# Band attention with a gated MLP on one core: negative tau through Q's scale, token sums on two engines, out products by column halves

## The chip, the cores and the metric

The kernel runs on 1 core of one Trainium2 chip. The time is that of the device, in microseconds (us), of one execution of the whole kernel; lower is better. The engines are named as in the profile: PE (TensorE, matrix products), PEld (its weight loads), DVE (VectorE), ACT (ScalarE), POOL (GpSimd) and SP (SyncE, which issues the DMAs).

## What is computed

The reference, cut to what matters:

```python
scale = 1.0 / np.sqrt(64)                                  # q, k, v: 8 batches, 8 heads, 576 rows, 64
scores = scale * q @ k^T
scores = where(scores >= max(scores) - tau, scores, -1e9)  # per row
attn = exp(scores - max(scores));  attn /= attn.sum() + 1e-9
x = (attn @ v).transpose(0, 2, 1, 3).reshape(4608, 512)
gate = sigmoid(x @ w_gate);  val = x @ w_val               # w: 512 x 1536
out = (gate * val) @ w_out                                 # 1536 x 512
```

Only scores within tau of the row's largest take part in the softmax. With a negative tau no score does, all are -1e9, and the row becomes the plain mean of v.

## The kernel before

**Attention.** There are 32 visits, one for each batch and pair of heads (name `b_hp`: `1_0` is batch 1, pair 0). A visit has 576 queries for each of two heads, in 9 tiles of 128 queries by 576 keys: four full tiles of each head, in groups of two, and one tile of both heads' 64 leftover queries. For each tile PE makes scores (L618), DVE their maximum (L625), ACT the exponent (L639), DVE masks and sums (L642; the sums land in a small tile `sm`). Then `normalise` (L665): the denominators are changed by `den_t` on ACT (L668), or on POOL (L671) in the first 18 tiles, DVE takes the reciprocal (L674), POOL computes (p + w_t) * sm (L687). `w_t` is 1 for a negative tau and 0 otherwise, and `den_t` is 576 * w_t + 1e-9, so that a negative tau gives the mean. PE transposes p (L702). In the first `NPV` = 4 visits the product with v is plain fp32 (L790). In the others p and v are split into a high and a low half (ACT rounds p to the high half, L712, DVE subtracts it, L719) and three cheaper products are summed (L803). The query scale goes into Q by ACT.

**The MLP**, all of it in such halves. The weights come through 36 conversions of a tile of 128 rows (`convert`, L401): among other steps three DVE operations (L441, L445, L451), a cast on ACT and a low half on POOL (L469), on DVE for the tiles in `DVE_LO_OUT`. Tokens of batches 0 to 4 run block by block (`in_units`: m, L861; `out_units`: o, L899). Batches 5 and 6, and 7 with all the leftovers, go as two token pairs, k = 0 and 1, through a scheme that makes four products of halves from seven (p1, p5, p6, p2, p7, p4, p3) of sums: weight sums on POOL (`sums`, from L940, spread by `SUMS` over the matmul units of earlier blocks), and token sums (`token_sums`, L993): `put` rounds a sum to its high half on ACT (L999) and DVE subtracts for the low one (L1001), `less` makes the next sum on POOL (L1006). `in_two` makes the q products (L1092; banks qa, qb, qc), `out_two` the r products (L1146; banks ra, rb, rc). Products p1 and p2 add up in bank a, p6, p7 and p4 in b, p5 and p3 in c; after a product DVE folds the bank into a partial result (`chains`, L1031 for r), before the next product of that bank may go on. In `out_two` a product has three groups g of two ff tiles, each with one load of weights (L1135), and two column halves e with banks of their own. The sums of every second product share buffers, so those of one are written when those of the one before are used up.

**What sets the order.** Every operation is handed to a planner (`Plan`) with its engine, an estimated cost and a key. It goes through time and gives each free engine the ready operation of the smallest key that finds a buffer (`SLOTS`), and so fixes one static instruction stream for each engine. Attention keys count tiles; MLP blocks come behind them on PE and fill what attention leaves free. `LEAD` is how far ahead a visit's loads and casts are keyed, `CONV_IN` the keys of the weight conversions (first, step), `SHIFT` an offset of the keys of all visits from the fifth on, `PAD` one more such number, `AHEAD_TWO` = 8 how many units before their use out weights may be loaded.

Of the kernel before, what the change touches and what calls it, by code (L numbers as in the profile page):

```python
# [19 lines left out]
def f32(ap):  # L20
    return ap.bitcast(F32)
# [21 lines left out]
class Plan:  # L43
# [157 lines left out]
    "w": 7, "t2": 5,  # L201
}
LEAD = 8
CONV_IN, CONV_OUT = (8, 2.2), (24, 3)
# [30 lines left out]

DEN_UNTIL = 18
NORM_ACT = ()
# [3 lines left out]
SHIFT = 30  # L241
# [6 lines left out]
DVE_LO_IN, DVE_LO_OUT = (), ()  # L248
# [9 lines left out]
SUMS = (36, 4)  # L258

AWAY = 1  # L260
AHEAD_TWO = 8


def act(n):
    return 0.19 + 0.0008 * n
# [15 lines left out]
def kernel(  # L281
# [57 lines left out]
    ntau_t = cp.tile([P, 1], F32, tag="ntau", name="ntau_t")  # L339


    w_t = cp.tile([P, 1], F32, tag="w", name="w_t")
    den_t = cp.tile([P, 2], F32, tag="den", name="den_t")
    nc.vector.tensor_scalar(out=w_t, in0=tau_t, scalar1=0.0, scalar2=None, op0=ALU.is_ge)
    nc.vector.tensor_scalar(out=w_t, in0=w_t, scalar1=-1.0, scalar2=1.0, op0=ALU.mult, op1=ALU.add)
    for i in range(2):
        nc.vector.tensor_scalar(
            out=den_t[:, i : i + 1], in0=w_t, scalar1=float(S), scalar2=1e-9, op0=ALU.mult, op1=ALU.add
        )
    nc.vector.tensor_scalar(out=ntau_t, in0=w_t, scalar1=1e38, scalar2=None, op0=ALU.mult)  # L350
    nc.vector.tensor_tensor(out=ntau_t, in0=ntau_t, in1=tau_t, op=ALU.subtract)
# [132 lines left out]
    class Visit:  # L484
# [39 lines left out]
        def split_scores(self, key, n):  # L524
# [15 lines left out]
            op("ACT", act(W), key, lambda: nc.scalar.activation(q2.ap[:, 0], qn.ap, AF.Copy, scale=QSCALE),  # L540
# [5 lines left out]
                out=q2.ap[:, 1], in0=qn.ap, scalar=QSCALE, in1=f32(q2.ap[:, 0]), op0=ALU.mult, op1=ALU.subtract  # L546
# [16 lines left out]
        def plain_scores(self, key, n):  # L563
# [17 lines left out]
            if len(heads) == 1:  # L581
                op("ACT", act(W), key, lambda: nc.scalar.activation(qn.ap, qn.ap, AF.Copy, scale=QSCALE), writes=[qn])
                return
            for i, c in enumerate((slice(0, WM), slice(WM, 2 * WM), slice(2 * WM, W))):
                op("ACT", act(c.stop - c.start), key, lambda c=c: nc.scalar.activation(
                    qn.ap[:, c], qn.ap[:, c], AF.Copy, scale=QSCALE
                ), writes=[(qn, i)])
# [59 lines left out]
    class Group:  # L647
        def __init__(self, vis, h, tiles):
# [7 lines left out]
            self.sm = buf("sm", [P, 2 * n], F32, f"sm{self.name}")  # L656
# [8 lines left out]
        def normalise(self, key):  # L665
            sm, p, n = self.sm, self.p, self.n
            if DEN(self.vis.first) == "ACT":
                op("ACT", 0.3, key, lambda: nc.scalar.activation(sm.ap[:, :n], sm.ap[:, :n], AF.Identity, bias=den_t[:, 0:1]),  # L668
                   writes=[sm])
            else:  # L670
                op("POOL", 0.3, key, lambda: nc.gpsimd.tensor_tensor(  # L671
                    out=sm.ap[:, :n], in0=sm.ap[:, :n], in1=den_t[:, :n], op=ALU.add
                ), writes=[sm])
            op("DVE", 0.17, key, lambda: nc.vector.reciprocal(out=sm.ap[:, :n], in_=sm.ap[:, :n]), writes=[sm])  # L674
            if NORM(self.vis.first) == "ACT":

                op("ACT", 0.3, key, lambda: nc.scalar.activation(
                    sm.ap[:, n:], sm.ap[:, :n], AF.Copy, scale=w_t[:, 0:1]
                ), writes=[sm])
                for i in range(n):  # L680
                    op("ACT", 0.74, key, lambda i=i: nc.scalar.activation(
                        p.ap[:, i * S : (i + 1) * S], p.ap[:, i * S : (i + 1) * S], AF.Identity,
# [519 lines left out]
    t = 0  # L1202
# [165 lines left out]
```

## Time and profile before

| what | value |
|---|---|
| median of 3 runs | 1405.61 us (1403.37 to 1407.85) |
| the profiled execution | 1396.95 us |
| its span, first to last instruction | 1395.2 us |
| TensorE clock granted in it | 0.999 |

One profiled execution gives, for each engine, which instruction ran when, how long, and what ended the idle time ahead of it. A row of a group reads: line, engine, operation, output <- input, shape, count | busy us, mean ns of one | idle us before, and which engine and line ended it. A row of the timeline reads: start, length, engine, line, what, [idle before <- who ended it]. "issue" is idle time that no recorded wait explains. Rows that take part in the argument are shown in the prediction.

### The profile page before, as it was taken

What the parts mean: (1) busy time and instruction counts of PE and PEld (TensorE: products, weight loads), DVE (VectorE), ACT (ScalarE), POOL (GpSimd) and SP (SyncE); (2) the same over time, 40 slices, a digit from 0 to 9 for tenths busy, and PEclk for the clock granted to TensorE, in tenths of its full rate; (3) what the DMA queues carried; (4) which work ended last, traced back from release to release, by engine and by line L of the source; (5) the groups of instructions that cost most, each with busy time, mean ns of one, the idle gap of its engine ahead of it and who ended that gap; (6) DMA issues with size and microseconds to landing.
All of it is one profiled execution on the core that took longest, in us unless ns stands there. A gap on an engine that the chain in (4) does not pass through costs nothing.

```text
span 1395.2 us, 23257 instructions
## 1 busy us (share of the span) xinstructions
PE 1357.9 (97%) x7472; PEld 1154.2 (83%) x7472; DVE 1097.0 (79%) x2144; ACT 875.3 (63%) x1930; POOL 801.4 (57%) x868
## 2 busy tenths in 40 slices
PE   7998999999999999999999999999999999899998
PEld 5666788888888888888888888888888887788886
DVE  7997989888788888888888888888936559645595
ACT  6877777677777777777777777777732235322242
POOL 5888765448787777786777976455420137001160
PEclk9999999999999999999999999999999999999999
DMA  7889888869999998899988999776567666665574
GB/s 266 279 248 314 303 260 238 230 205 264 267 261 330 292 278 250 261 289 296 304 267 242 303 295 277 200 224 198 160 223 227 201 195 202 202 199 187 184 225 137
DMA packets 142328, 341.28 MB, mean 245 GB/s; under 512 B 22784, under 2 KB 42752, under 8 KB 142208
## 3 DMA queue, kind: packets, MB, share of 16 engines
q1 hardware_dynamic: 142064, 339.80, 79.8%
q8 instruction: 61, 1.00, 0.3%
q14 instruction: 59, 0.48, 0.1%
q10 hardware_dynamic: 144, 0.00, 0.0%
HBM read 232.78 MB, written 55.57 MB: 207 GB/s over the span
## 4 chain that ended last, share of the span: by engine, by line
PE 78%; DMA 6%; DVE 6%; POOL 3%; ACT 2%; issue 2%; SPq 1%; DVEq 0%; ACTq 0%; POOLq 0%
PE m L861 17%; PE o L899 11%; PE s L618 9%; PE av L803 8%; PE qb L1092 7%; PE tp L702 6%; PE qa L1092 4%; PE qc L1092 4%; DMA su<-wid 4%; PE rb L1146 3%; PE av L790 2%; PE ra L1146 2%; PE rc L1146 2%; PE s_l L618 2%; POOL su L947 1%
## 5 line engine op out<-in xcount | busy, mean ns | idle before, releaser
L861 PE MATMUL m<-x,wi 128*128 128x512 f32 x1152 | 314.0, 403 | 0.0
L687 POOL TENSOR_SCALAR p<-p,w_t,sm 128x576 f32<-128x576 f32 x256 | 216.8, 857 | 91.5 <-DVE sm L674 80.7
L861 PEld LDWEIGHTS m<-x,wi 128*128 128x128 f32 x1152 | 200.9, 189 | 30.9
L642 DVE SCALAR_TENSOR_TENSOR p<-s,st,p 128x576 f32<-128x576 f32 x256 | 206.2, 812 | 23.0 <-ACT p L639 18.6
L625 DVE TENSOR_REDUCE st<-s 128x1 f32<-128x576 f32 x256 | 190.4, 751 | 34.1 <-PE s L618 30.1
L899 PE MATMUL o<-g,wo 128*128 128x512 f32 x720 | 194.3, 403 | 0.0
L639 ACT ACTIVATE p<-s,st 128x576 f32<-128x576 f32 x256 | 188.8, 738 | 6.9 <-DVE st L625 5.4
L712 ACT CAST pt<-tp 128x512 fp32r<-128x512 f32 x224 | 128.2, 587 | 63.5 <-PE tp L702 59.4
L719 DVE TENSOR_TENSOR pt<-tp,pt 128x512 fp32r<-128x512 f32 x224 | 150.5, 684 | 18.3 <-ACT pt L712 16.3
L618 PE MATMUL s<-kd,qd 128*128 128x288 f32 x896 | 159.7, 301 | 4.9 <-DVE p L642 2.7
L618 PEld LDWEIGHTS s<-kd,qd 128*128 128x128 f32 x896 | 136.8, 188 | 23.0 <-issue 3.0
L702 PE MATMUL tp<-ident,p 128*128 128x128 f32 x1024 | 146.8, 273 | 1.9 <-ACT pl_l L737 1.4
L899 PEld LDWEIGHTS o<-g,wo 128*128 128x128 f32 x720 | 126.1, 189 | 20.6 <-PE tp_l L702 0.2
L803 PE MATMUL av<-pt,vs 128*128 128x320 f32 (+1 forms) x896 | 137.0, 295 | 1.7 <-DVE pt L719 1.7
L702 PEld LDWEIGHTS tp<-ident,p 128*128 128x128 f32 x1024 | 122.3, 140 | 19.1 <-issue 3.2
L803 PEld LDWEIGHTS av<-pt,vs 128*128 128x128 f32 x896 | 129.2, 188 | 9.1 <-POOL p L687 2.1
L1006 POOL TENSOR_TENSOR gA<-gA 128x512 f32<-128x512 f32 x12 | 16.2, 1347 | 206.4 <-DVE gA L1071 206.4
L883 POOL TENSOR_TENSOR g<-th,g 128x512 fp32r<-128x512 f32 x60 | 78.8, 1313 | 23.0 <-ACT g L881 21.4
L806 ACT COPY avt<-av 64x256 f32<-64x256 f32 x112 | 44.2, 394 | 58.2 <-PE av L803 56.4
L1029 DVE TENSOR_TENSOR qu<-qb,qp 128x512 f32<-128x512 f32 x48 | 33.2, 691 | 55.9 <-PE qb L1092 48.4
L807 DVE TENSOR_TENSOR xf<-av,avt 64x256 f32<-64x256 f32 x112 | 50.8, 453 | 32.3 <-ACT avt L806 31.1
L749 DVE TENSOR_TENSOR pl<-lk,pl 64x128 fp32r<-64x128 f32 x224 | 64.7, 289 | 13.8 <-ACT pl L746 7.3
(171 smaller groups left out, 2743.1 us busy)
## 6 DMA issues: line engine op xcount, KB each, us to landing
wi<-wid SPq DMA_DIRECT2D x96, 512.0 KB, 7.1
kd<-k SPq DMA_DIRECT2D x112, 320.0 KB, 8.1
wo<-wod SPq DMA_DIRECT2D x60, 512.0 KB, 7.6
qd<-q SPq DMA_DIRECT2D x112, 128.0 KB, 6.1
wid<-ws SPq DMA_DIRECT2D x24, 512.0 KB, 4.5
su<-wid SPq DMA_DIRECT2D x24, 512.0 KB, 7.9
sid<-su SPq DMA_DIRECT2D x24, 512.0 KB, 4.6
wa<-wid SPq DMA_DIRECT2D x24, 512.0 KB, 4.5
```

The lines of the kernel that those rows point to most:

```text
L618: nc.tensor.matmul(s.ap[:, c, :HALF], st(), mv(slice(k0 + c * HALF, k0 + (c + 1) * HALF)), start=m == 0, stop=m == len(steps) - 1,)
L625: op("DVE", 0.76, key, lambda: nc.vector.tensor_reduce(out=st.ap[:, 0:1], in_=sv(), axis=AX.XY, op=ALU.max, negate=True), reads=[s], write ...
L639: op("ACT", 0.74, key, lambda: nc.scalar.activation(p(), sv(), AF.Exp, bias=st.ap[:, 0:1], scale=1.0), reads=[s, (st, 0)], writes=[(g.p, i)])
L642: op("DVE", 0.9, key, lambda: nc.vector.scalar_tensor_tensor(out=p(), in0=sv(), scalar=st.ap[:, 1:2], in1=p(), op0=ALU.is_ge, op1=ALU.mult ...
L687: op("POOL", 0.9, key, lambda i=i: nc.gpsimd.tensor_scalar(out=p.ap[:, i * S : (i + 1) * S], in0=p.ap[:, i * S : (i + 1) * S], scalar1=w_t ...
L702: nc.tensor.matmul(tp.ap[:, c, :], self.p.ap[:, o + c * P : o + (c + 1) * P], ident, is_transpose=True, start=c == 0, stop=c == NJ - 1, sk ...
L712: op("ACT", 0.58, key, lambda: nc.scalar.copy(hi(), tp.ap), reads=[tp], writes=[(self.pt, (0, i))])
L719: op("DVE", 0.69, key, lambda: nc.vector.tensor_tensor(out=lo(), in0=tp.ap, in1=f32(hi()), op=ALU.subtract), reads=[tp, (self.pt, (0, i))] ...
L803: nc.tensor.matmul(av.ap, st, mv, start=i == 0, stop=i == len(ms) - 1)
L861: nc.tensor.matmul(m.ap, wv[:, a, c * P : (c + 1) * P], xs[c].ap[:, z, c0:c1], start=e == 0, stop=e == 11,)
L899: nc.tensor.matmul(acc.ap, wv[:, f, a], g[fg * ND + f].ap[:, z], start=(fg, f, a, z) == (0, 0, 0, 0), stop=(fg, f, a, z) == (NFG - 1, ND - ...
L1092: nc.tensor.matmul(acc.ap, wv[:, y, (2 * h + c) * P : (2 * h + c + 1) * P], xt[prod][c].get()[:, z], start=e == 0 and prod in FIRST, stop= ...
```

## The change

Scale and denominators: Q is multiplied by a `[128, 1]` tile `scale_t` (the query scale for tau >= 0, else 0), so that a negative tau makes all scores 0 and every one passes the threshold 0; `ntau_t` is -max(tau, 0). `w_t` and `den_t` go, and with them L668, L671 and the second operand of L687; the reciprocal follows L642 directly. Token sums: the low halves (L1001) take their engine in turn, DVE, DVE, POOL. `out_two`: a product issues its three loads first, and all products but p1 then run column half by column half. One more visit (1_0) has the plain fp32 product with v (`NPV`). A third partial of the chains lies in the slot `pc` where it lay in `t2`, and `t2` has 6 slots. The weight sums come once in 6 units, three low halves of out weights go to DVE, and `LEAD`, `CONV_IN`, `PAD` and `SHIFT` have other values, by which the planner orders anew. Dead code goes.

```diff
@@ SLOTS and numbers @@
-    "w": 7, "t2": 5,
+    "w": 7, "t2": 6,
-LEAD = 8
-CONV_IN, CONV_OUT = (8, 2.2), (24, 3)
+LEAD = 3
+CONV_IN, CONV_OUT = (12, 2.2), (24, 3)
-PAD = 56
-NPS, NPV = 4, 4
+PAD = 64
+NPS, NPV = 4, 5
-SHIFT = 30
+SHIFT = 20
-DVE_LO_IN, DVE_LO_OUT = (), ()
+DVE_LO_IN, DVE_LO_OUT = (), range(6, 12, 2)
-SUMS = (36, 4)
+SUMS = (36, 6)
+TURNS = ("DVE", "DVE", "POOL")
@@ setup @@
-    nc.vector.tensor_scalar(out=w_t, in0=tau_t, scalar1=0.0, scalar2=None, op0=ALU.is_ge)
-    nc.vector.tensor_scalar(out=w_t, in0=w_t, scalar1=-1.0, scalar2=1.0, op0=ALU.mult, op1=ALU.add)
...
+    nc.vector.tensor_scalar(out=ntau_t, in0=tau_t, scalar1=0.0, scalar2=-1.0, op0=ALU.max, op1=ALU.mult)
+    nc.vector.tensor_scalar(out=scale_t, in0=tau_t, scalar1=0.0, scalar2=QSCALE, op0=ALU.is_ge, op1=ALU.mult)
@@ Visit.prepare (the same for qn.ap, and as the scalar of q2's low half on DVE) @@
-            op("ACT", act(W), key, lambda: nc.scalar.activation(q2.ap[:, 0], qn.ap, AF.Copy, scale=QSCALE),
+            op("ACT", act(W), key, lambda: nc.scalar.activation(q2.ap[:, 0], qn.ap, AF.Copy, scale=scale_t[:, 0:1]),
@@ Group.normalise @@
-            if DEN(self.vis.first) == "ACT":
-                op("ACT", 0.3, key, lambda: nc.scalar.activation(sm.ap[:, :n], sm.ap[:, :n], AF.Identity, bias=den_t[:, 0:1]),
-                   writes=[sm])
...
-            op("DVE", 0.17, key, lambda: nc.vector.reciprocal(out=sm.ap[:, :n], in_=sm.ap[:, :n]), writes=[sm])
+            op("DVE", 0.17, key, lambda: nc.vector.reciprocal(out=sm.ap, in_=sm.ap), writes=[sm])
             for i in range(n):
                 op("POOL", 0.9, key, lambda i=i: nc.gpsimd.tensor_scalar(
-                    out=p.ap[:, i * S : (i + 1) * S], in0=p.ap[:, i * S : (i + 1) * S], scalar1=w_t[:, 0:1], scalar2=sm.ap[:, i : i + 1],
-                    op0=ALU.add, op1=ALU.mult,
+                    out=p.ap[:, i * S : (i + 1) * S], in0=p.ap[:, i * S : (i + 1) * S],
+                    scalar1=sm.ap[:, i : i + 1], scalar2=None, op0=ALU.mult,
                 ), reads=[sm], writes=[(p, i)])
@@ token_sums, put @@
-            op("DVE", 0.69, key, lambda: nc.vector.tensor_tensor(
+            e = next(turns)
+            op(e, {"DVE": 0.69, "POOL": 1.3}[e], key, lambda: {"DVE": nc.vector, "POOL": nc.gpsimd}[e].tensor_tensor(
                 out=to.get()[:, 1], in0=src.get(), in1=f32(to.get()[:, 0]), op=ALU.subtract
@@ chains @@
-        t = {c: buf("pc" if c == "u3" and tag == "q" else "t2", [P, SM], F32, f"{tag}{c}{n}") for c in ("p1", "u2", "u3")}
+        t = {c: buf("pc" if c == "u3" and not (tag == "r" and n.endswith("_1")) else "t2", [P, SM], F32, f"{tag}{c}{n}") for c in ("p1", "u2", "u3")}
@@ out_two @@
         for prod in SEVEN:
+            ws = []
             for g in range(NFG):
                 w = buf("w", [P, 2, 2, 2, P], F32R, f"wo2{k}_{prod}_{g}")
...
-                for e in range(2):
+                ws.append(w)
+            for g, e in [(g, e) for g in range(NFG) for e in range(2)] if prod == "p1" else [(g, e) for e in range(2) for g in range(NFG)]:
+                if True:
+                    w = ws[g]
                     bank, t, after = quads[e]
...
                     if g == NFG - 1:
                         after(prod)
-                unit_ends.append(end)
+                if e or prod != "p1":
+                    unit_ends.append(end)
```

How this moves instructions shows at three places. First, PE in the first pair's output products, where p7 ends and p4 begins (rb0_0 and rb0_1 are bank b of column halves 0 and 1; gs0_p7_* are token sums of product p7, q2 and ptc being its last two; wo20_p7_1 the weights of group 1). Before:

```order
L1146 MATMUL rb0_0_14752<-gs0_p7_q2_14824,wo20_p7_2_14805 128x512 x3
L1146 MATMUL rb0_0_14752<-gs0_p7_ptc_14830,wo20_p7_2_14805 128x512 x3
L1146 MATMUL rb0_0_14752<-gs0_p4_0_14846,wo20_p4_0_14826 128x512 x3
L1146 MATMUL rb0_0_14752<-gs0_p4_1_14850,wo20_p4_0_14826 128x512 x3
L1146 MATMUL rb0_0_14752<-gs0_p4_2_14866,wo20_p4_1_14848 128x512 x3
L1146 MATMUL rb0_0_14752<-gs0_p4_3_14870,wo20_p4_1_14848 128x512 x3
L1146 MATMUL rb0_0_14752<-gs0_p4_4_14883,wo20_p4_2_14868 128x512 x3
L1146 MATMUL rb0_0_14752<-gs0_p4_5_14887,wo20_p4_2_14868 128x512 x3
L1146 MATMUL rb0_1_14767<-gs0_p7_0_14782,wo20_p7_0_14761 128x512 x6
L1146 MATMUL rb0_1_14767<-gs0_p7_1_14803,wo20_p7_1_14784 128x512 x6
```

The bank rb0_0 goes from p7 straight to p4. Changed:

```order
L1121 MATMUL rb0_0_14512<-gs0_p7_q2_14679,wo20_p7_2_14593 128x512 x3
L1121 MATMUL rb0_0_14512<-gs0_p7_ptc_14683,wo20_p7_2_14593 128x512 x3
L1121 MATMUL rb0_1_14553<-gs0_p7_1_14584,wo20_p7_1_14590 128x512 x6
L1121 MATMUL rb0_1_14553<-gs0_p7_q2_14679,wo20_p7_2_14593 128x512 x3
L1121 MATMUL rb0_1_14553<-gs0_p7_ptc_14683,wo20_p7_2_14593 128x512 x3
L1121 MATMUL rb0_0_14512<-gs0_p4_0_14629,wo20_p4_0_14644 128x512 x3
L1121 MATMUL rb0_0_14512<-gs0_p4_1_14632,wo20_p4_0_14644 128x512 x3
L1121 MATMUL rb0_0_14512<-gs0_p4_2_14642,wo20_p4_1_14646 128x512 x3
L1121 MATMUL rb0_0_14512<-gs0_p4_3_14648,wo20_p4_1_14646 128x512 x3
```

Between the end of p7 in rb0_0 and the start of p4 there now stand 12 matmuls of rb0_1.

Second, POOL in the same stage (gA and gB are gated activations of which `less` makes sums, gs their halves, xb and xs those of the second pair's tokens). Before:

```order
L1006 TENSOR_TENSOR gA0_5_14200<-gB0_5_14222,gA0_5_14200 128x512
L1006 TENSOR_TENSOR gA0_8_14338<-gB0_8_14360,gA0_8_14338 128x512
L1006 TENSOR_TENSOR gA0_9_14477<-gB0_9_14499,gA0_9_14477 128x512
L1006 TENSOR_TENSOR xb1_2_0_13795<-xb1_2_0_13795,xb1_0_0_13431 128x512
L1006 TENSOR_TENSOR gB0_0_13823<-gB0_0_13823,gA0_0_13793 128x512
L1006 TENSOR_TENSOR gB0_1_13945<-gB0_1_13945,gA0_1_13923 128x512
L1006 TENSOR_TENSOR gB0_4_14083<-gB0_4_14083,gA0_4_14061 128x512
L1006 TENSOR_TENSOR gB0_5_14222<-gB0_5_14222,gA0_5_14200 128x512
L1006 TENSOR_TENSOR gB0_8_14360<-gB0_8_14360,gA0_8_14338 128x512
L1006 TENSOR_TENSOR gB0_9_14499<-gB0_9_14499,gA0_9_14477 128x512
L1006 TENSOR_TENSOR xb1_3_0_13762<-xb1_3_0_13762,xb1_1_0_13741 128x512
```

Changed, the second part of it:

```order
L972 TENSOR_TENSOR gs0_p2_3_14527<-gB0_5_14018,gs0_p2_3_14527 128x512
L977 TENSOR_TENSOR gB0_5_14018<-gB0_5_14018,gA0_5_13996 128x512
L977 TENSOR_TENSOR gB0_8_14156<-gB0_8_14156,gA0_8_14134 128x512
L972 TENSOR_TENSOR gs0_p7_1_14584<-gA0_4_13857,gs0_p7_1_14584 128x512
L977 TENSOR_TENSOR gA0_9_14273<-gB0_9_14295,gA0_9_14273 128x512 x2
L977 TENSOR_TENSOR gB0_9_14295<-gB0_9_14295,gA0_9_14273 128x512
L972 TENSOR_TENSOR xs1_p2_0_14392<-xb1_2_0_13529,xs1_p2_0_14392 128x512
L972 TENSOR_TENSOR gs0_p4_1_14632<-gB0_1_13741,gs0_p4_1_14632 128x512
L972 TENSOR_TENSOR gs0_p4_4_14658<-gB0_8_14156,gs0_p4_4_14658 128x512
L977 TENSOR_TENSOR xb1_2_0_13529<-xb1_2_0_13529,xb1_0_0_13177 128x512
L977 TENSOR_TENSOR xb1_3_0_13501<-xb1_3_0_13501,xb1_1_0_13477 128x512
L972 TENSOR_TENSOR gs0_p7_ptc_14683<-gA0_9_14273,gs0_p7_ptc_14683 128x512
```

Low halves (L972) now stand between the sums (L977), and the last low half of p7 (gs0_p7_ptc) is POOL's, behind two sums for the second pair.

Third, SP where block 0's gate and value weights end (wid11_1 is the last of these tiles in DRAM, wi0_11_1a its load for block 0, qd1_3 and kd1_3 the scaled queries and keys of visit 1_3, in pieces). Before:

```order
L474 DMA wid11_1_131<-ws11_1_2495 128x1024
L840 DMA wi0_11_0a_2532<-wid11_0_130 128x1024
L555 DMA qd1_3_0_2615<-q21_3_2605 64x512
L840 DMA wi0_11_1a_2623<-wid11_1_131 128x1024
L559 DMA kd1_3_0_2630<-k21_3_2595 64x2x640 x2
L528 DMA kn2_0_2642<-in_k_dram 128x640
L840 DMA wo0_0_0_2660<-wod0_132 128x1024
L534 DMA qn2_0_2673<-in_q_dram 128x640
L555 DMA qd1_3_0_2615<-q21_3_2605 64x512
L555 DMA qd1_3_1_2704<-q21_3_2605 64x512 x2
```

Changed:

```order
L808 DMA wi0_10_1a_2550<-wid10_1_124 128x1024
L808 DMA wi0_11_0a_2605<-wid11_0_125 128x1024
L501 DMA vn2_0_2620<-in_v_dram 128x640
L1222 DMA xa1_1_139<-xf1_1_2176 128x512
L1229 DMA xp1_1_135<-xf1_1_2176 256x1x32
L460 DMA wid11_1_126<-ws11_1_2597 128x1024
L808 DMA wi0_11_1a_2719<-wid11_1_126 128x1024
L520 DMA qn2_0_2730<-in_q_dram 128x640
L541 DMA qd1_3_0_2385<-q21_3_2372 64x512
L808 DMA wo0_0_0_2744<-wod0_127 128x1024
L541 DMA qd1_3_1_2510<-q21_3_2372 64x512
```

The write of wid11_1 now stands directly ahead of the load that waits for it, with a piece of qd1_3_0 two rows behind that load; before, two rows lay between write and load, and that piece stood five behind.

More of the change, by code (lines that the diff above doesn't have):

```diff
@@ L1 @@
 import heapq
+import itertools
 from contextlib import ExitStack
@@ L339 @@
     ntau_t = cp.tile([P, 1], F32, tag="ntau", name="ntau_t")
-    w_t = cp.tile([P, 1], F32, tag="w", name="w_t")
-    den_t = cp.tile([P, 2], F32, tag="den", name="den_t")
-    nc.vector.tensor_scalar(out=w_t, in0=tau_t, scalar1=0.0, scalar2=None, op0=ALU.is_ge)
-    nc.vector.tensor_scalar(out=w_t, in0=w_t, scalar1=-1.0, scalar2=1.0, op0=ALU.mult, op1=ALU.add)
[L346 to L351, printed above, removed]
+    nc.vector.tensor_scalar(out=ntau_t, in0=tau_t, scalar1=0.0, scalar2=-1.0, op0=ALU.max, op1=ALU.mult)
+    scale_t = cp.tile([P, 1], F32, tag="scale", name="scale_t")
+    nc.vector.tensor_scalar(out=scale_t, in0=tau_t, scalar1=0.0, scalar2=QSCALE, op0=ALU.is_ge, op1=ALU.mult)
     least_t = cp.tile([P, 1], F32, tag="least", name="least_t")
```

29 lines of the change are left out of this document (5 added, 24 removed).

## The prediction, made before the changed kernel ran

> **What bounds the kernel now.** I read the page's first lines, the chain of work that ended last, the busy time by stretches, and the waits of TensorE in each stretch.
>
> ```profile
> span 1395.2 us, 23257 instructions
> PE 1357.9 (97%) x7472; PEld 1154.2 (83%) x7472; DVE 1097.0 (79%) x2144; ACT 875.3 (63%) x1930; POOL 801.4 (57%) x868
> PE 78%; DMA 6%; DVE 6%; POOL 3%; ACT 2%; issue 2%; SPq 1%; DVEq 0%; ACTq 0%; POOLq 0%
> ```
>
> TensorE (PE) is busy for 1357.9 of 1395.2 us and has 78% of the chain. So two things move the time: TensorE work that is added or dropped, and the 37.3 us in which it is not busy. To place those, the windows; columns are the stretch, its length, busy us of PE, PE's weight loads, DVE, ACT and POOL (instructions in brackets), TensorE clock, DMA share and GB/s.
>
> ```profile
> 0.00:125.00 125.00, 109.03 (x591) 75.37 (x592) 105.00 (x216) 95.82 (x185) 97.16 (x142) 1.00 0.80 269
> 125.00:200.00 75.00, 71.53 (x380) 59.97 (x381) 66.17 (x129) 53.87 (x117) 54.83 (x56) 0.98 0.92 296
> 200.00:1030.00 830.00, 824.46 (x4960) 730.01 (x4959) 698.94 (x1508) 616.73 (x1444) 558.99 (x610) 1.00 0.87 255
> 1030.00:1150.00 120.00, 118.56 (x523) 97.59 (x522) 64.50 (x92) 31.71 (x55) 25.16 (x19) 1.00 0.67 220
> 1150.00:1222.00 72.00, 66.42 (x288) 53.12 (x287) 58.87 (x67) 29.61 (x52) 28.89 (x18) 1.00 0.65 208
> 1222.00:1329.00 107.00, 107.00 (x474) 88.60 (x473) 55.13 (x81) 24.01 (x41) 12.90 (x10) 1.00 0.60 191
> 1329.00:1396.00 67.00, 60.94 (x267) 49.54 (x265) 48.41 (x54) 23.55 (x41) 23.49 (x14) 0.99 0.54 173
> ```
>
> Idle PE time is 16.0 us up to 125 us, 3.5 up to 200, 5.5 in the long middle, 1.4 up to 1150, 5.6 in the first output stage of the token pairs, nothing in the next stretch, and 6.1 at the end, most of it the tail behind the last matmul. More than the sum of these is not to be had without less matmul work. Their causes, as the waits of PE in five of those stretches (total us, times, longest; first 125 to 200, then 1030 to 1150, 1150 to 1222, 1329 on):
>
> ```profile
> PE m L861 <- DVE th L877: 1.9, 2, 1.1
> PE s L618 <- DVE p_l L642: 1.4, 1, 1.4
> PE s L618 <- DVE p L642: 0.7, 1, 0.7
> ```
>
> ```profile
> PE qb L1092 <- DVE qu L1029: 1.4, 1, 1.4
> ```
>
> ```profile
> PE rb L1146 <- issue: 1.7, 1, 1.7
> PE rb L1146 <- ACT gs_p L999: 1.3, 1, 1.3
> PE rc L1146 <- DMA wo_p<-sod: 1.1, 1, 1.1
> PE rb L1146 <- DVE gs_p_ptc L1001: 0.7, 1, 0.7
> PE rb L1146 <- DVE gs_p_q L1001: 0.6, 1, 0.6
> ```
>
> ```profile
> PE rb L1146 <- issue: 0.8, 1, 0.8
> PE rc L1146 <- DMA wo_p<-sod: 0.7, 1, 0.7
> ```
>
> Is the busy time full? A stretch without a wait answers.
>
> ```profile
> 1050.00:1100.00 50.00, 50.00 (x222) 41.40 (x221) 28.22 (x42) 11.52 (x19) 5.15 (x4) 1.00 0.65 213
> ```
>
> 222 matmuls in 50 us are 225 ns each with no gap; so it is full there, and added matmuls cost their whole time. (The Trainium skill, Perfetto Trace Analysis, § Identifying the Most-Contended Engine, has it that TensorE's headroom is judged by the weight loads' busy share and not by matmul busy time; by their 83% some 17% would be free, the visit's 6.1 us below would vanish in it, and the sum would be 12.7 us gained instead of 6.6. In this stretch the loads stand at the same 41.40 / 50 = 83% while PE never waits, so here that share is the full one.)
>
> **The change part by part.**
>
> *One more visit (1_0) with plain fp32 probabilities times values.* It adds PE work. Two rows of the chain (start, us) and two of the timeline:
>
> ```profile
> 18.66 2.44 PE av L790 x10
> ...
> 26.76 3.02 PE av L790 x20
> ```
>
> ```profile
> 1018.04 1.11 PE L803 MATMUL av<-pt,vs 128*128 128x256 f32 x8
> ...
> 1022.89 1.33 PE L803 MATMUL av<-pt,vs 128*128 128x320 f32 x8
> ```
>
> Plain, a group takes 2.44 us, with the leftovers 3.02; split, 1.11 and 1.33. A visit has two of each: 10.92 against 4.88, so **+6.1 us**, all on the full engine. DVE loses the low halves of that visit, which only helps if DVE is waited for.
>
> *The head.* The first MoE matmul, the point from which PE has filler, waits for 20 to 22 weight tiles converted on DVE.
>
> ```profile
> L441 DVE TENSOR_SCALAR wb<-wa 128x512 int32<-128x512 int32 x36 | 24.7, 686 | 2.4 <-POOL wa L428 2.0
> ...
> L451 DVE SCALAR_TENSOR_TENSOR wa<-wr,wb 128x512 int32<-128x512 int32 x36 | 24.6, 683 | 0.7
> ```
>
> ```profile
> 125.70 7.00 PE L861 MATMUL m<-x,ws 128*128 128x512 f32 x24
> ```
>
> By the instruction order, 22 conversions stand on DVE ahead of the last probabilities of the fourth visit before, 20 after; three operations of 0.68 to 0.69 each make 2.06 us, so 4.1 us less, and that visit's chain ends earlier by it. PE stands at the same row when the first m comes. Attention work does not shrink, so only idle time of the 16.0 us can go. Bounds 0 (another engine ends it) and −5.5 (the two conversions, and the POOL and ACT steps that leave with them); I take **−4.0**, by the DVE row.
>
> *125 to 200.* DVE ends 4.0 us of waits (1.9 + 1.4 + 0.7); conversions and the visit's low halves leave DVE there. Bounds 0 and −4.1; I take **−3.0**.
>
> *The middle.* The adding of the denominators leaves ACT, and the weight sums come one per 6 units, not 4.
>
> ```profile
> L668 ACT ACTIVATE sm<-sm,den_t 128x2 f32<-128x2 f32 x120 | 35.6, 297 | 5.8 <-DVE p L642 5.0
> ```
>
> ```profile
> qd<-q SPq DMA_DIRECT2D x112, 128.0 KB, 6.1
> ...
> wid<-ws SPq DMA_DIRECT2D x24, 512.0 KB, 4.5
> ```
>
> ACT loses 120 × 0.30 = 36 us here (and 30 shorter ones), but it is not the bound, and this stretch has 5.5 us of idle PE in 830; so at most −4. Against it, at the end of block 0's gate and value weights SP issues the write of the last tile, waiting for POOL, then the load back, waiting for that write to land (4.5 us), and behind these the last piece of qd1_3_0. PE takes that piece some 80 instructions, about 7 us, later, and it takes 6.1 us to land: a stall of 0 to 3, and other late loads 1 more. Bounds −4 and +4; I take **−1.0**, nearer to nothing than to either end, since cover on PE is filler in all of it. The scale as a pointer on ACT and DVE, the multiply without an add on POOL (one operation either way) and the low halves of three out weights on DVE instead of POOL (3 × 0.7 us) lie beside this full PE: nothing. Without the cover the last costs 2 us.
>
> *Before the first token pair.* 21.3 us of block matmuls now lie between the last attention work and the first q product (14.0 before), and the chains have one slot more. The 1.4 us wait for DVE goes: **−1.5** (bounds 0, −1.6).
>
> *The first output stage.* A product now runs all its groups for one column half, then the other. Before, bank rb went from its p7 to its p4 at once, and PE waited for the turn of the bank.
>
> ```profile
> 1195.19 0.68 DVE L1031 SCALAR_TENSOR_TENSOR ru<-rb,rp 128x512 f32<-128x512 f32 x1
> ...
> 1195.96 7.07 PE L1146 MATMUL rb<-gs_p,wo_p 128*128 128x512 f32 x30 [1.69 <-issue]
> ```
>
> Now the other half's p7, 12 matmuls of 225 ns = 2.7 us, lies between, more than the 1.7 us turn. That wait goes. The rest, 5.6 − 1.7 = 3.9 us, hangs on the sums. A third of their low halves moves from DVE to POOL:
>
> ```profile
> 1134.07 0.68 DVE L1001 TENSOR_TENSOR gs_p_q<-gA,gs_p_q 128x512 fp32r<-128x512 f32 x1
> ...
> 1140.33 1.29 POOL L1006 TENSOR_TENSOR gA<-gB,gA 128x512 f32<-128x512 f32 x1
> ...
> 1154.63 1.78 DVE L1001 TENSOR_TENSOR gs_p_ptc<-gA,gs_p_ptc 128x512 fp32r<-128x512 f32 x1
> ```
>
> ```profile
> 1159.40:1191.60 32.20, 23.29 (x14) 1.00 0.64 198
> ```
>
> (The last row is the window of line 1006 on POOL.) A DVE operation of 0.68 us takes 1.78 beside a POOL one, and POOL's 14 take 23.29 / 14 = 1.66 each where one alone takes 1.29. In the stretch from the second half-sum of gA to p7's last low half POOL has 23 operations in the new order for 14: at 1.3 to 1.65 us, 30 to 38 us from about 1161, so 1191 to 1199; PE wants that low half at about 1190. So a new wait of 1 to 9 us can come, and the 5.6 of now can go. I take **−1.7**: the bank's turn gone, the sums as late as now; bounds −5.6 and +3 (the new wait at its middle, 5, less the 1.7).
>
> (The Trainium skill, GPSIMD Engine Reference, § Specifications, states that GpSimd shares its SBUF interfaces with VectorE, with contention for DVE instructions that read two inputs in SBUF. By that, moving a low half frees less DVE time than its row says; the trace agrees, with 0.68 to 1.78.)
>
> *The second output stage* has less of other work; the same bank's turn (0.8) and a load's wait (0.7, now issued a product's length earlier) go: **−1.5** (bounds 0, −1.5).
>
> Sum: +6.1 − 4.0 − 3.0 − 1.0 − 1.5 − 1.7 − 1.5 = **−6.6 us**. The profiled execution took 1396.95 us, its span 1395.2, so it would take 1390.3. The three timed runs had a median of 1405.61 (1403.37 to 1407.85), 8.7 above; I take off the same 6.6: **1399.0**. A measurement here can tell from no change about 0.3%, 4.2 us.
>
> **Rivals.**
>
> *Slower: DVE is not what the head waits for.* If the first m stands at 125.7 again because ACT, POOL or the loads (DMA share 0.80 there) are as late, a lighter DVE is worth nothing before 200 us, nor in the waits that name DVE later. Then +6.1 stands against the −1.5 of the second output stage, which is order alone: +4.6, 1410.2. It decides if the first m moves by less than about 2 us. For it: ACT 95.82 and POOL 97.16 of 125 us are nearly as busy as DVE's 105.00. Against it: DVE ends the larger waits behind it.
>
> *POOL becomes the bound of the first output stage.* At 1.65 us each the low halves of p7 come 9 us late; the other half's p7 hides 2.7 of it, and of the 6 left some falls in waits that are there now; with +2.5 in place of the −1.7 the sum is −2.4, 1403.2. For it: 23 × 1.65 = 38 us in a stretch of about 31. Against: POOL idles 72 − 28.89 us there now, and TensorE goes on with the other half while one is late.
>
> *More than forecast.* If the waits before 200 us fall whole (−5.5, −4.1), the middle gives its −4 and the first output stage −5.6: with +6.1, −1.6 and −1.5 the ends make −16.2; all but the middle's 2, −14, 1391.6. For it: every one of these waits names an engine that gets lighter.
>
> *The change does not do what it says.* A planner orders the work, and could undo the grouping or the earlier conversions. The printed order speaks against it at the three places above; if so, within 0.3%.
>
> **How the numbers follow.** Chances: forecast 0.45 (of it 0.35 beyond 0.3%), more than forecast 0.20, slower 0.17 (of it 0.11 beyond 0.3%, since any small gain brings it back), POOL 0.12 (0.03 beyond), no effect 0.06. Faster by over 0.3% (under 1401.4): 0.35 + 0.20 + 0.03 = 0.58; slower (over 1409.8): 0.11; within: 0.31. The range runs from 1389, where the larger gain still stands, to 1411, just past the slower rival's own sum; what is left out is about 0.2.
>
> **What would show it.** Right: the first m at about 121 to 122 us, PE idle 12 us before 125 in place of 16; visit 1_0's plain products about 3 us each; no wait of rb for issue in either output stage; waits of 125 to 200 below 2 us. Wrong: the first m at 124 or later; new waits of rb for POOL's low halves over 4 us; a wait of s for the load qd1_3_0 near the end of block 0's conversions above 2 us; PE idle in the middle above 8.

## The result, and the profile after

The changed kernel takes 1462.65 us (median of 4 runs, 1461.47 to 1464.13), the kernel before in the same runs 1404.93 (1403.37 to 1407.85): a ratio of 1.0409, with a 95% interval of 1.0388 to 1.043. It is 57.7 us slower. 1399.0 was forecast, with a range of 1389 to 1411. The profiled execution took 1461.47 us.

The page of the changed kernel, first the span and the engines, then the costliest group on POOL; the last line is the same group on the page of the kernel before:

```profile
span 1459.6 us, 23131 instructions
PE 1381.5 (95%) x7500; PEld 1155.1 (79%) x7500; DVE 1087.6 (75%) x2084; ACT 850.1 (58%) x1775; POOL 1096.5 (75%) x887
L655 POOL TENSOR_SCALAR p<-p,sm 128x576 f32<-128x576 f32 x256 | 443.0, 1740 | 42.4 <-DVE sm L653 39.3
```

```profile
L687 POOL TENSOR_SCALAR p<-p,w_t,sm 128x576 f32<-128x576 f32 x256 | 216.8, 857 | 91.5 <-DVE sm L674 80.7
```

DVE and ACT got lighter, as the diff says. POOL went from 801.4 to 1096.5 us. Most of that is one line: the normalising multiply, L655, takes 1740 ns where L687 took 857. With the 32 operations on the leftover tiles, a row of their own, that is 498.9 us for 243.3, so 255.6 of the 295.1 us more. (The low halves that POOL took over, L972, add 57.4; other lines lose a little.) In the kernel before this line was the same operation with `+ w_t` in front; the change took one of its two operations away.

The windows of the changed kernel, in the columns of the prediction's:

```profile
0.00:125.00 125.00, 103.17 (x514) 68.71 (x515) 91.37 (x187) 81.77 (x148) 105.71 (x114) 0.99 0.65 222
125.00:200.00 75.00, 65.76 (x365) 49.23 (x364) 55.98 (x101) 52.50 (x102) 65.81 (x54) 1.00 0.86 275
200.00:1030.00 830.00, 795.82 (x4733) 693.06 (x4732) 682.46 (x1456) 574.39 (x1266) 744.95 (x597) 1.00 0.84 252
```

From 200 to 1030 us POOL (the last of the five engines) is now busy for 744.95 of 830 us, 90%, where it was 558.99, and TensorE is idle for 34.2 us where it was 5.5. The stretches after 1030 us don't line up with those of before, since everything comes later. (The chain breaks off after 14% of the span and isn't read.) What TensorE waits for, the five longest:

```profile
PE tp L670 <- POOL p L655: 35.5, 41, 2.9
PE s L604 <- DVE p L628: 11.1, 12, 2.3
PE tp L670 <- DVE xf L775: 4.1, 2, 3.6
PE rb L1121 <- DVE ru L1002: 3.6, 1, 3.6
PE s_l L604 <- DVE p L628: 3.0, 2, 1.7
```

The transposes wait for POOL's p in 41 places, 35.5 us; before, no such wait stood in the list. How one comes about, in the timeline of POOL, then of PE, of the changed kernel:

```profile
617.72 1.29 POOL L915 TENSOR_TENSOR su<-su 128x512 f32<-128x512 f32 x1 [0.75 <-DMA su<-wid]
619.00 1.72 POOL L655 TENSOR_SCALAR p<-p,sm 128x576 f32<-128x576 f32 x1
```

```profile
617.33 2.52 PE L829 MATMUL m<-x,wi 128*128 128x512 f32 x10
620.77 0.66 PE L670 MATMUL tp<-ident,p 128*128 128x128 f32 x4 [0.91 <-POOL p L655]
```

POOL runs one instruction behind another, so the multiply starts when a weight sum is done and ends at 620.72; PE's stream has the transposes next and stands still until 620.77. The planner, which placed the filler ahead of them, reckons 0.9 us for this operation, in both kernels.

### The profile page after: what moved, and what is told of

It is laid out like the page before. It is cut to its first block, busy times and chain, and to the rows that moved or that the text cites. A ratio compares the mean times of both kernels' runs of the same rounds, so it can differ in the third digit from the quotient of the medians.

```text
span 1459.6 us, 23131 instructions
## 1 busy us (share of the span) xinstructions
PE 1381.5 (95%) x7500; PEld 1155.1 (79%) x7500; DVE 1087.6 (75%) x2084; ACT 850.1 (58%) x1775; POOL 1096.5 (75%) x887
## 5 line engine op out<-in xcount | busy, mean ns | idle before, releaser
L655 POOL TENSOR_SCALAR p<-p,sm 128x576 f32<-128x576 f32 x256 | 443.0, 1740 | 42.4 <-DVE sm L653 39.3
L611 DVE TENSOR_REDUCE st<-s 128x1 f32<-128x576 f32 x256 | 189.9, 752 | 36.9 <-PE s L604 34.2
L867 PE MATMUL o<-g,wo 128*128 128x512 f32 x720 | 198.7, 404 | 0.0
L625 ACT ACTIVATE p<-s,st 128x576 f32<-128x576 f32 x256 | 188.4, 738 | 15.7 <-DVE st L611 14.3
L670 PE MATMUL tp<-ident,p 128*128 128x128 f32 x1024 | 152.7, 276 | 40.0 <-POOL p L655 35.5
L670 PEld LDWEIGHTS tp<-ident,p 128*128 128x128 f32 x1024 | 119.3, 140 | 75.6 <-POOL p L655 54.6
L687 DVE TENSOR_TENSOR pt<-tp,pt 128x512 fp32r<-128x512 f32 x216 | 146.0, 687 | 34.6 <-ACT pt L680 29.9
L680 ACT CAST pt<-tp 128x512 fp32r<-128x512 f32 x216 | 124.3, 586 | 81.2 <-PE tp L670 76.7
L771 PE MATMUL av<-pt,vs 128*128 128x320 f32 (+1 forms) x864 | 133.0, 296 | 1.3 <-DVE pt L687 1.3
L771 PEld LDWEIGHTS av<-pt,vs 128*128 128x128 f32 x864 | 124.1, 189 | 8.1 <-DVE pt L687 1.8
L977 POOL TENSOR_TENSOR gA<-gA 128x512 f32<-128x512 f32 x12 | 16.3, 1362 | 134.1 <-DVE gA L1042 134.1
L851 POOL TENSOR_TENSOR g<-th,g 128x512 fp32r<-128x512 f32 x60 | 78.1, 1302 | 17.9 <-ACT g L849 13.2
L616 ACT ACTIVATE st<-st,ntau_t 128x1 f32<-128x1 f32 x224 | 66.1, 295 | 24.9 <-DVE st L611 23.2
L1063 PE MATMUL qa<-xs_p,wa 128*128 128x512 f32 x288 | 73.1, 389 | 0.0
```

Of the source, the lines that this page charges most:

```text
L611: op("DVE", 0.76, key, lambda: nc.vector.tensor_reduce(out=st.ap[:, 0:1], in_=sv(), axis=AX.XY, op=ALU.max, negate=True), reads=[s], write ...
L625: op("ACT", 0.74, key, lambda: nc.scalar.activation(p(), sv(), AF.Exp, bias=st.ap[:, 0:1], scale=1.0), reads=[s, (st, 0)], writes=[(g.p, i)])
L655: op("POOL", 0.9, key, lambda i=i: nc.gpsimd.tensor_scalar(out=p.ap[:, i * S : (i + 1) * S], in0=p.ap[:, i * S : (i + 1) * S], scalar1=sm. ...
L670: nc.tensor.matmul(tp.ap[:, c, :], self.p.ap[:, o + c * P : o + (c + 1) * P], ident, is_transpose=True, start=c == 0, stop=c == NJ - 1, sk ...
L680: op("ACT", 0.58, key, lambda: nc.scalar.copy(hi(), tp.ap), reads=[tp], writes=[(self.pt, (0, i))])
L687: op("DVE", 0.69, key, lambda: nc.vector.tensor_tensor(out=lo(), in0=tp.ap, in1=f32(hi()), op=ALU.subtract), reads=[tp, (self.pt, (0, i))] ...
```

## The experiments

**1. The form of POOL's operation.** Two theories. A: the form with one operation is slow by itself, and that is the loss. B: the new order, and the low halves that POOL took over, keep POOL company, and the row is long for that. Run e1 gives the operation its old form (`zero_t` is a `[128, 1]` tile of zeros) and leaves the order of all engines as it is:

```diff
-                    scalar1=sm.ap[:, i : i + 1], scalar2=None, op0=ALU.mult,
+                    scalar1=zero_t[:, 0:1], scalar2=sm.ap[:, i : i + 1], op0=ALU.add, op1=ALU.mult,
```

> The changed kernel with the normalising operation on POOL in the form that it had before: (p + zero) * reciprocal, zero being a [128, 1] tile of zeros in place of w_t. The order of all instructions stays. Theory A (the form with the multiply alone costs 1740 ns in place of 857, and that is the whole loss): POOL's row falls back to 850 to 870 ns, the wait of the transposes for POOL (35.5 us) goes, and the time is what the prediction's other steps make, 1395 to 1405. Theory B (the new order and POOL's added low halves make POOL late, and the row is long because of the company it has): the row stays above 1200 ns, or the time stays above 1430.

Run e2 puts a second operation that does nothing behind the multiply; e3 reads its 1.0 from a tile.

```diff
-                    scalar1=sm.ap[:, i : i + 1], scalar2=None, op0=ALU.mult,
+                    scalar1=sm.ap[:, i : i + 1], scalar2=1.0, op0=ALU.mult, op1=ALU.mult,
```

> The changed kernel with a second operation that changes nothing: (p * reciprocal) * 1.0, the 1.0 as a number in the instruction. It tells apart two readings of theory A. A1 (one operation alone is the slow form): the row is 850 to 870 ns and the time within 3 us of the run with (p + zero). A2 (a multiply first, by a pointer, is the slow form, or a number as the second operand is): the row stays at 1700 ns or more and the time at 1455 to 1470. Theory B: 1455 to 1470 too, with a row above 1200.

> As the run before, with the 1.0 read from a [128, 1] tile, so that two pointers are read as in the kernel before, with a multiply as the first operation in place of an add. A1, and any reading by which two pointers are the fast form: 850 to 870 ns. If a multiply as the first operation is what is slow: 1700 or more. If a number is as good as a pointer, this and the run before agree within 20 ns.

Run e4 does the reverse, in the kernel before:

```diff
-                    out=p.ap[:, i * S : (i + 1) * S], in0=p.ap[:, i * S : (i + 1) * S], scalar1=w_t[:, 0:1], scalar2=sm.ap[:, i : i + 1],
-                    op0=ALU.add, op1=ALU.mult,
+                    out=p.ap[:, i * S : (i + 1) * S], in0=p.ap[:, i * S : (i + 1) * S],
+                    scalar1=sm.ap[:, i : i + 1], scalar2=None, op0=ALU.mult,
```

> The kernel before with one thing changed: POOL's normalising operation is p * reciprocal alone, without the + w_t (which is 0 for this tau, so the results stay for it; a negative tau is no longer handled). Theory A: the row goes from 857 to 1720 to 1750 ns, POOL gets 288 x 0.88 = 250 us more, and the time rises by about as much as between the two kernels, or more by what the rest of the change gives: 1455 to 1475. Theory B (order and company): the row stays below 1000 ns and the time at 1400 to 1410.

| run | median, us | ratio to the kernel before | 95% interval |
|---|---|---|---|
| changed kernel | 1462.65 | 1.0409 | 1.0388 to 1.043 |
| e1, (p + zero) * r | 1403.55 | 1.0003 | 0.9981 to 1.0026 |
| e2, (p * r) * 1.0 | 1403.34 | 0.9986 | 0.9966 to 1.0006 |
| e3, as e2 by two pointers | 1403.87 (one run) | | |
| e4, before with p * r alone | 1466.88 | 1.0459 | 1.0432 to 1.0487 |

The same row of each of the four profiles, e1 to e4 in turn:

```profile
L655 POOL TENSOR_SCALAR p<-p,zero_t,sm 128x576 f32<-128x576 f32 x256 | 212.3, 837 | 88.3 <-DVE sm L653 81.5 <-PE tp L670 3.7 <-PE av L771 1.8
```

```profile
L655 POOL TENSOR_SCALAR p<-p,sm 128x576 f32<-128x576 f32 x256 | 191.8, 760 | 92.5 <-DVE sm L653 85.8 <-PE tp L670 3.9 <-PE av L771 1.8
```

```profile
L655 POOL TENSOR_SCALAR p<-p,sm,one_t 128x576 f32<-128x576 f32 x256 | 212.3, 838 | 87.6 <-DVE sm L653 80.9 <-PE tp L670 3.7 <-PE av L771 1.8
```

```profile
L687 POOL TENSOR_SCALAR p<-p,sm 128x576 f32<-128x576 f32 x256 | 445.0, 1749 | 39.4 <-DVE sm L674 37.9 <-DVE sm_l L674 1.4
```

Theory A holds both ways: with a second operation, whichever it is, the row falls to 760 to 838 ns and the loss is gone; without one, the kernel before loses as much as the changed one, or a little more (4.6% against 4.1%). The waits say the same: in e1 none of the transposes waits for POOL's p any more, in e4 they wait for it in 35 places, 27.1 us. B falls with e1, which has the changed kernel's order and low halves and neither its row nor its time. Among the readings of A, a multiply in front is not what is slow (e2, e3), and the second operand may be a number. e1 and e3, with two pointers, take 77 to 78 ns more than e2 with one; all three had been expected at 850 to 870 ns, and are faster.

**2. What makes the form slow.** Run e11 puts 28 operations on a tile of ones in front of the kernel, four for each of seven forms, one line each (and takes one slot of `t2` to make room). `sx` is the tile, `h` its left half of 288 columns, `sp1` a `[128, 1]` tile of ones; `...` stands for the loop line in front of each, and the line numbers are added here:

```diff
+    for _ in range(4):
+        nc.gpsimd.tensor_scalar(out=sx, in0=sx, scalar1=sp1[:, 0:1], scalar2=None, op0=ALU.mult)   # L338
...
+        nc.gpsimd.tensor_scalar(out=sx, in0=sx, scalar1=1.0, scalar2=None, op0=ALU.mult)           # L340
...
+        nc.gpsimd.tensor_scalar(out=sx, in0=sx, scalar1=sp1[:, 0:1], scalar2=None, op0=ALU.max)    # L342
...
+        nc.gpsimd.tensor_scalar(out=h, in0=h, scalar1=sp1[:, 0:1], scalar2=None, op0=ALU.mult)     # L344
...
+        nc.gpsimd.tensor_scalar(out=sx, in0=sx, scalar1=1.0, scalar2=1.0, op0=ALU.mult, op1=ALU.mult)           # L346
...
+        nc.gpsimd.tensor_scalar(out=sx, in0=sx, scalar1=sp1[:, 0:1], scalar2=1.0, op0=ALU.mult, op1=ALU.mult)   # L348
...
+        nc.gpsimd.tensor_scalar(out=h, in0=h, scalar1=sp1[:, 0:1], scalar2=1.0, op0=ALU.mult, op1=ALU.mult)     # L350
```

> The base with 28 more operations on POOL at its start, four of each form on a [128, 576] tile of ones, to price the forms by themselves; one slot of t2 less to make room. Each line of the seven is one form. A1 (one operation alone is slow, whatever it is and wherever its operand comes from): multiply by a pointer, multiply by a number and maximum by a pointer alike near 1720 ns, the two-operation lines near 760; at 288 columns half of each. A3 (only a single multiply by a pointer is slow): 1720 in the first line, 760 in the second and third. A4 (the slow form has a fixed cost of some 900 ns): at 288 columns 1300 in place of 860.

The seven groups of that profile:

```profile
L338 POOL TENSOR_SCALAR sx<-sx,sp 128x576 f32<-128x576 f32 x4 | 6.9, 1724 | 0.4
L342 POOL TENSOR_SCALAR sx<-sx,sp 128x576 f32<-128x576 f32 x4 | 6.9, 1718 | 0.4
L340 POOL TENSOR_SCALAR sx<-sx 128x576 f32<-128x576 f32 x4 | 6.6, 1648 | 0.3
L344 POOL TENSOR_SCALAR sx<-sx,sp 128x288 f32<-128x288 f32 x4 | 4.0, 1003 | 0.4
L348 POOL TENSOR_SCALAR sx<-sx,sp 128x576 f32<-128x576 f32 x4 | 3.0, 745 | 0.4
L346 POOL TENSOR_SCALAR sx<-sx 128x576 f32<-128x576 f32 x4 | 2.7, 671 | 0.3
L350 POOL TENSOR_SCALAR sx<-sx,sp 128x288 f32<-128x288 f32 x4 | 2.0, 504 | 0.4
```

A1 holds, for the two operations tried: one alone is slow, multiply or maximum, and wherever its operand comes from. So A3 falls, and A4 with it: what one operation costs beyond two is 499 ns at 288 columns and 979 at 576, so it grows with the width and isn't fixed. Between 288 and 576 columns the time is (1724 - 1003) / 288 = 2.50 ns a column with one operation and (745 - 504) / 288 = 0.84 with two, so three times as much, with some 280 and 260 ns that don't depend on the width. No other engine does anything from 20 to 36.5 us, so nothing keeps the last four groups that ran (L344 to L350) company. Why the chip takes longer for one operation than for two, no run here shows. (The operations hold POOL from 1.9 to 36.5 us, so the run's 1432.27 us says nothing here.)

**3. What the rest of the change is worth.** From here e2 (1403.3 us) is the base: the changed kernel without its slow form. The forecast had 6.6 us less than before for it; its interval is 4.8 us less to 0.8 more. Four runs take one part back each.

```diff
-TURNS = ("DVE", "DVE", "POOL")
+TURNS = ("DVE",)
```

> The changed kernel with (p * reciprocal) * 1.0 (the base from here on, 1403.3 us) and all low halves of the token sums back on DVE. Theory P (POOL's third of the low halves slows the others on DVE, and so the turn of bank rb comes 3.5 us late): the wait of rb for DVE's L1002 falls below 1 us, DVE's row of L972 in the first output stage falls from 36.79 us for 24 (1.53 each), and the time falls by 2 to 6 us. Theory Q (the moved third is relief for DVE, as its giver meant): the waits of rc and rb for DVE's L972 grow by 2 to 6 us and the time with them.

```diff
-            for g, e in [(g, e) for g in range(NFG) for e in range(2)] if prod == "p1" else [(g, e) for e in range(2) for g in range(NFG)]:
+            for g, e in [(g, e) for g in range(NFG) for e in range(2)]:
```

> The base with the output products by groups as before the change (each group's two column halves behind one another). By the forecast's term for the bank's turn, 0 to 4 us more in the two output stages together, shown as a wait of rb between p7 and p4; by the rival (the order by column halves only moves waits) within 1.5 us of the base.

```diff
-NPS, NPV = 4, 5
+NPS, NPV = 4, 4
```

> The base with visit 1_0 split again (four plain visits, not five). If the plain product costs its matmul time on a full TensorE, as forecast: 6 us less than the base, 1397 to 1398, TensorE's busy time before 1030 us 6 us less. If the split visit's DVE work (about 10 us) was what it saved: equal to the base or up to 5 us more, with longer waits for DVE's p and first m later than 125 us.

```diff
-LEAD = 3
-CONV_IN, CONV_OUT = (12, 2.2), (24, 3)
+LEAD = 8
+CONV_IN, CONV_OUT = (8, 2.2), (24, 3)
...
-PAD = 64
+PAD = 56
...
-SHIFT = 20
+SHIFT = 30
```

> The base with the planner's numbers LEAD, CONV_IN, PAD and SHIFT of the kernel before. If they bring the gain in the head that was forecast (4.0 and 3.0 us): 1408 to 1411, first m at 129 us or later. If they bring nothing there: 1401 to 1406.

And three combine the edits above: e9 the first and the third, e10 the first two, e12 all of the first three.

> The base with both parts back that lost alone: four plain visits and all low halves of the token sums on DVE. If the two gains add (4.7 and 1.9 us beside the base's 1403.3): 1396 to 1398, a ratio to the kernel before of 0.993 to 0.995, faster than both kernels. If the split visit's new waits (4.2 us for ACT's pt and 3.5 of issue) come back in full or grow: 1399 to 1402.

> The base with all low halves on DVE and the output products by groups, to price the order by column halves without POOL's share. If it is worth the forecast's 1.7 and 1.5 us by itself: 2 to 4 us above the run with the low halves on DVE alone (1398.6), so 1400.5 to 1402.5, with a wait of rb between p7 and p4. If it had its worth only because POOL's low halves came late (the run by groups lost 6.7 us with 8.9 us of wait for POOL): within 1.5 us of 1398.6.

> The base with all three parts back: four plain visits, all low halves on DVE, output products by groups. What is left of the change is the query scale and the bare reciprocal, the loads of a product issued together, the slots, the spread of the weight sums and the planner's numbers. If the order by column halves has worth of its own: 1 to 3 us above the run with the first two parts back (ratio 0.990), so 0.991 to 0.993. If the order is worth nothing once POOL has no low halves: a ratio of 0.988 to 0.991. If the three do not add: above 0.993.

| run | median, us | ratio to the kernel before | 95% interval |
|---|---|---|---|
| e2, base | 1403.34 | 0.9986 | 0.9966 to 1.0006 |
| e5, low halves on DVE | 1398.60 | 0.9951 | 0.9927 to 0.9975 |
| e6, by groups | 1410.09 | 1.0045 | 1.0023 to 1.0066 |
| e7, four plain visits | 1401.47 | 0.9979 | 0.996 to 0.9999 |
| e8, planner's old numbers | 1407.45 | 1.003 | 1.0006 to 1.0053 |
| e9, e5 and e7 together | 1392.58 | 0.9901 | 0.9872 to 0.993 |
| e10, e5 and e6 together | 1395.10 | 0.9915 | 0.9885 to 0.9945 |
| e12, all three | 1391.54 | 0.9905 | 0.988 to 0.9929 |

*The low halves* (e5). Theory P holds: DVE alone is better, by 4.7 us (the two intervals overlap by a thousandth). Its place is the first output stage, 1150 to 1222 us, where TensorE is idle for 2.6 us where the base has 7.5. (The whole span of the e5 profile, 1398.4 us, doesn't show it: that execution was its slowest, 1400.56 us, with a clock of 0.95 in the first 125 us.) DVE's and POOL's busy time in line 972 from 1150 to 1222 us, of the base, then of e5, which has DVE alone:

```profile
1150.00:1222.00 72.00, 44.00 (x32) 25.12 (x16) 0.98 0.59 190
```

```profile
1150.00:1222.00 72.00, 49.65 (x51) 1.00 0.64 207
```

Sixteen low halves on POOL took 25.12 us of POOL and left DVE with 32 at 44.00 / 32 = 1.38 us each; DVE alone does 51 at 49.65 / 51 = 0.97. So DVE got rid of a third of the operations and of 5.7 us, 11%. (The window's ends cut 48 operations out of one run and 51 out of the other.) (That is the row of the prediction, 0.68 us alone and 1.78 beside POOL, at work; by the rule that the prediction cites from the Trainium skill, GPSIMD Engine Reference, § Specifications, a low half on DVE, which reads two tiles, and work on POOL get in each other's way; the trace agrees, with the 1.38 us here against 0.97.) What PE waits for longest in the base, in the timeline of DVE and PE:

```profile
1189.10 5.14 DVE L972 TENSOR_TENSOR gs_p<-gB,gs_p 128x512 fp32r<-128x512 f32 x3
...
1194.16 0.68 DVE L1002 SCALAR_TENSOR_TENSOR ru<-rb,rp 128x512 f32<-128x512 f32 x1
...
1194.89 5.30 PE L1121 MATMUL rb<-gs_p,wo_p 128*128 128x512 f32 x15 [3.55 <-DVE ru L1002]
```

The turn of bank rb, 0.68 us, stands on DVE behind three low halves that take 5.14 us instead of 2.0, and TensorE waits 3.55 us for it. By the order of the products it is the turn from p6 to p7, not that from p7 to p4. In e5 that wait is gone; the waits of both output stages are these two:

```profile
PE rc L1121 <- DVE gs_p L972: 3.3, 5, 0.7
PE rb L1121 <- DVE gs_p_ptc L972: 0.7, 1, 0.7
```

*The order by column halves* (e6, e10, e12). By itself, taken back in the base, it loses 6.7 us, more than expected, but the wait is not that of the bank:

```profile
PE rc L1121 <- POOL gs_p L972: 8.9, 1, 8.9
PE ra L1121 <- POOL gs_p L972: 2.7, 1, 2.7
```

By the order of the products those are a low half of p5, in the first output stage, and one of p2, in the second, both POOL's. Once DVE makes them all, both orders take the same within the intervals (e10 against e5, where e10 is even 3.5 us lower, which was not expected, and e12 against e9), and no wait of rb for the bank's turn shows in either output stage of e10: the planner, with other inputs, put the other half's p7 in between there too. So in these versions the order is worth nothing that could be measured, and what it is worth in the base hangs on POOL's late halves. Whether it covers them or the planner only places them later in the other order, isn't told apart.

*The fifth plain visit* (e7). TensorE's busy time falls from 1365.5 to 1361.2 us, but the median only by 1.9, less than the 6 of one reading, where the other had no gain. Two waits that the base hasn't come up in the first 200 us:

```profile
PE av L758 <- ACT pt L677: 4.2, 2, 2.5
...
PE s L604 <- issue: 3.5, 1, 3.5
```

Others get shorter there (that of s for DVE's p from 8.0 to 3.9), and over the whole profile TensorE's idle time rises from 33.0 to 38.3 us. The first MoE matmul (m) comes at 130.85 us; in e9 and e12, without the fifth plain visit too, it comes at 133.09 and 132.18. With that visit it comes at 125.02 to 128.80 (e1, e2, e3, e5, e6 and e10, whose order up to there is the same). So the plain visit buys an earlier filler with its matmul time. With the low halves on DVE the same edit goes along with 1398.60 to 1392.58 (ratios 0.9951 and 0.9901, whose intervals just overlap), more than the 1396 to 1398 of the two gains added, and from e10 to e12 with nothing sure (0.9915 and 0.9905). That it saves between nothing and 6 us is all that these runs show.

*The planner's numbers* (e8) are worth about 4 us (1.003 against 0.9986; the intervals touch), with a wait of 2.4 us for a load of qd among what comes back. The time lies between the two ranges that were expected. The first m stands at 125.02 us in the base and 125.20 with the old numbers, not at 129 or later, so the gain isn't where the forecast had it.

e9 and e12 beat both kernels: 1392.58 and 1391.54 us, by 0.7 to 1.3% over the kernel before.

## Why the prediction was wrong

**The step that failed** is in the middle's paragraph: "the multiply without an add on POOL (one operation either way) ... lie beside this full PE: nothing". Both halves of it were wrong. The operation that is left isn't the one of before at less work; it costs 1740 ns for 857 (e4 shows it in the kernel before, e11 apart from everything). And 288 of them at 0.88 us more are 254 us of POOL, which the full PE doesn't cover: 236 of the 288 lay in the middle's 830 us, where 208 more on top of 559 make POOL busy for 92%, and it came to 90%. The price wasn't bounded from both sides there, though no row of the trace showed the form at any width. POOL's rows of one operation lie on both sides of the old 857 ns: by columns, a cast (614 ns at 512) would give 691 ns at 576, and the low half of 128 x 640 (1593 ns) 1434. The dear end would have made a rival of 166 us more work on POOL, and even that is short of what was measured.

**No rival held it.** The slower one had DVE not being what the head waits for; the POOL one was put in the first output stage, for another reason, at +2.5 us in place of -1.7.

**The loss in terms.** Against the base, which has the same 7500 matmuls, the span grows by 1459.6 - 1398.5 = 61.1 us: TensorE's idle time from 33.0 to 78.1, and its busy time by 16.0. The matmuls themselves take hardly longer (by count and mean of their rows 2608 us against 2603), so they overlap less, and short gaps between them must be counted as busy.

**The other terms**, with the slow form taken out (e2 against before, one profile each, TensorE idle by the windows; e2's span ends at 1398.5 us, in the last of them):

```profile
0.00:125.00 125.00, 110.67 (x594) 76.83 (x595) 103.69 (x207) 92.33 (x171) 85.99 (x127) 0.99 0.77 256
125.00:200.00 75.00, 71.61 (x395) 57.58 (x394) 59.63 (x113) 52.57 (x108) 49.89 (x52) 1.00 0.94 299
200.00:1030.00 830.00, 827.52 (x4964) 731.83 (x4963) 699.69 (x1507) 593.34 (x1311) 543.83 (x615) 1.00 0.86 257
1030.00:1150.00 120.00, 120.00 (x531) 99.39 (x531) 63.44 (x88) 32.64 (x56) 32.05 (x24) 1.00 0.67 224
1150.00:1222.00 72.00, 64.55 (x271) 51.36 (x270) 55.34 (x49) 28.11 (x50) 53.35 (x34) 0.98 0.59 190
1329.00:1410.00 81.00, 64.13 (x281) 52.16 (x279) 46.56 (x44) 24.19 (x42) 41.83 (x26) 0.98 0.47 155
```

| term | forecast, us | measured, us | |
|---|---|---|---|
| plain visit, PE busy | +6.1 | +7.6 | 1365.5 - 1357.9, other busy time in it |
| head | -4.0 | -1.6 | idle 16.0 to 14.3; first m at 125.02, not 121 to 122 |
| 125 to 200 | -3.0 | -0.1 | the three waits shown 4.0 to 3.4; that of s for DVE's p grew, 0.7 to 2.0 |
| middle | -1.0 | -3.1 | idle 5.5 to 2.5; no stall for qd_3 |
| before the first pair | -1.5 | -1.4 | right |
| first output stage | -1.7 | +1.9 | idle 5.6 to 7.5; POOL's rival, at about its size |
| second output stage | -1.5 | +0.1 | the wait for the bank gone, one of 1.6 for the sums new |

They add up to +3.4 (the spans give +3.3) where -6.6 was forecast. Parts of 1 to 3 us are within what one execution differs from another: the profile of e1, with the same order on every engine, has a span of 1402.0 us. The head was mis-sized in any case: the first m stands 0.7 us earlier in e2 than before (125.70), but 1.6 to 3.1 later in the five other profiles with the same order up to there, and never 2 us earlier, from where the slower rival would have been out. DVE's busy time up to 125 us fell by only 1.3 us, it stays the busiest engine there beside TensorE (103.69 of 125 us), and the waits of s for DVE's p in the first 200 us are 8.0 us. What ends the head otherwise wasn't tried. The first output stage (64.55 us of busy time in e1 too) went as the POOL rival said, and by e5 for its reason, though the wait came at the bank's turn from p6 to p7, behind slowed low halves on DVE, not at p7's last low half. The turn from p7 to p4 is hidden, as forecast: in the base the last three matmuls of p7 start at 1204.12 us and the 36 of p4 at 1204.80, with no idle time between. In the timed runs, with their wider spread, base and before can't be told apart.

**Whether added matmuls are hidden**, as the share of weight loads would have it, isn't decided: e7 took 4.3 us of busy time away, and the idle time rose by 5.3.

## What to carry to other kernels

Taking an operation out of an instruction can make the instruction slower: when an edit changes an instruction's form, price the new form from a row that shows it, and where there is none, bound it by the nearest rows before calling it free. When an engine's busy time jumps, look at its rows by mean time first; the busy shares say where the time went only after that. Work moved to an engine beside which the first one runs slower frees less than its row says: here a third of the operations for 11% of the time.

## What the runs showed of the hardware

On POOL, a tensor-scalar operation in fp32 on 128 partitions costs 2.50 ns for each column between 288 and 576 with one arithmetic operation and 0.84 ns with two. At 576 columns that is 1648 to 1724 ns, whether the one operation multiplies or takes a maximum and whether its operand is a pointer or a number, against 671 and 745. A second operation that does nothing, a multiply by 1.0, is worth 980 ns there, and 59 us in this kernel. All the cases were in place, in fp32; other types, and an output in another tile, weren't tried. The operand's kind costs little beside that: 74 to 76 ns for a pointer in place of a number.
